# Moving query tiles into the kv stage and output weights to another queue in a fused gated-mix kernel

## The chip, the cores and the metric

The kernel runs on one core of one Trainium2 chip. The metric is the device time of one execution in microseconds (us); where several executions were measured, the median is given. A profiled execution records every instruction of every engine, with the clock that was granted to TensorE; positions in it are given in us from the start of its span.

## The reference, cut to what matters

The input is one sequence of S = 2048 tokens with D = 512 features in bf16. Two branches are computed from it and mixed by a gate:

```python
g = sigmoid((x * gate_w).sum(-1, keepdims=True))
# A: linear attention, 32 heads of width 16
q, k, v = split(x @ wqkv)
pq, pk = q @ w_phi, k @ w_phi                        # per head
phi_q = concat(softmax(pq), softmax(-pq))            # 32 features
phi_k = concat(softmax(pk), softmax(-pk))
kv, z = phi_k^T v, sum_s phi_k                       # over all tokens
a = ((phi_q kv) / (phi_q z + 1e-6)) @ wo
# B: gated MLP that mixes tokens
zz = gelu(x @ w_in); z1, z2 = zz[:, :688], layernorm(zz[:, 688:])
b = (z1 * (w_sp @ z2 + b_sp)) @ w_out
out = g * a + (1 - g) * b
```

## The kernel before, in words

The tokens are cut into 16 tiles of 128 rows. The kernel has three stages.

**The z stage** (to about 49 us) computes both gelu halves of branch B (`z_mm`, line 184) and the layer norm of the second, and folds `w_phi` into the query and key weights.

**The kv stage** (lines 495 to 513, from about 49 to 120 us) loops over the 16 tiles. An iteration computes the key features of the next tile (`k_tile`: four matmuls on line 318, two exps on ScalarE on line 322, the softmax sums on VectorE on line 326, reciprocals and a ratio, and a rescaling of the negative half on GpSimd on line 335), the values of this tile (`v_tile`, lines 358 to 363), adds the kv product of the tile two iterations back into one accumulator (`kv_acc`, line 374), and computes one "spatial half" of branch B (`gg_next`: 16 matmuls on line 410 for one half of the columns of one tile of `w_sp @ z2`, then the gating by z1 on VectorE on line 415). After both halves of a tile the product is transposed by a DMA transpose (`u_T`, line 441). Iterations 13 and 15 also compute a query tile (`q_tile`): the same steps as a key tile and then a DMA transpose into `eqT` (line 352). After the loop, the last kv products are added and the accumulator is masked into `kvz` (lines 380 and 385).

**The output stage** (lines 516 to 527) first loads the output weights (`load_out_weights`: a memset on GpSimd and five DMA loads into one tile, `slabs`, which takes the space of the key and value weights). Then 16 slots follow. Slot i computes query tile i+2, one spatial half, attention tile i (`attn_tile`: eight matmuls on line 423, the division on VectorE on lines 426 and 428, a DMA transpose of the result on line 436), and in odd slots from 3 on the output of a pair of tiles (`ba_pair`: for each tile four matmuls on line 447 with `wo`, five on line 449 and a last one on line 452 with `w_out`, a scaling on ScalarE, and the store). The last two output tiles stand alone, the last one in two halves of the columns.

What sets the order: TensorE and ScalarE run in the order of the code (`manual_schedule`). On VectorE, GpSimd and SP a scheduler fixes the order when the kernel is built; each engine then runs its own list strictly in order, the DMA issues on SP's and ScalarE's lists among the rest. All DMA transposes are on SP. Buffers are rings: six PSUM banks for `mm`, one accumulator shared by `kvacc` and `at`, two buffers for `eq`, four for `eqT`, ten for `uT`, four for `oT`, four for the gate products `ucat`. A writer waits until its buffer's last reader is done.

Of the kernel before, what the change touches and what calls it, by code (L numbers as in the profile page):

```python
# [11 lines left out]
BF16 = mybir.dt.bfloat16  # L12
I32 = mybir.dt.int32

P = 128
# [5 lines left out]
FH = 688  # L21
HF = FH // 2
NT = S // P
# [3 lines left out]
NFT = (FH + P - 1) // P  # L27
# [3 lines left out]
REM = FH - 5 * P  # L31
# [4 lines left out]
def kernel(  # L36
# [14 lines left out]
    nc = tc.nc  # L51
# [15 lines left out]
    wq_p = pers.tile([P, NDT, D], BF16, name="wq_p")  # L67
# [39 lines left out]
        out=ramp[:, 0, :], data0=ones32[:, :], data1=zeros[:, :], initial=0.0,  # L107
# [4 lines left out]
    for q in range(4):  # L112
        qs = slice(32 * q, 32 * q + 32)
        nc.vector.tensor_tensor(
            out=ident[qs, qs], in0=ramp[qs, 0, :], in1=ramp[qs, 1, :], op=ALU.is_equal)
    nc.gpsimd.dma_start(out=gaterow[:, :], in_=gate_w.rearrange("(dt p) -> dt p", p=P))
    nc.gpsimd.dma_start(out=brow[:, :], in_=B_b_sp.rearrange("(t p) -> t p", p=P))
    def load_z2w(eng, dt):
# [9 lines left out]
        out=xs[:, 2:4, :], in_=x2[2 * P:4 * P, :].rearrange("(i p) d -> p i d", p=P))  # L128
    for h in range(2):
        nc.sync.dma_start(  # L130
            out=w_z1[:, 2 * h:2 * h + 2, :], in_=w_in_v[:, 2 * h:2 * h + 2, 0:FH])
    for i in range(4, 8):
        nc.sync.dma_start_transpose(out=xT[:, :, i * P:(i + 1) * P], in_=x2[i * P:(i + 1) * P, :])
    for q in range(2, NCH):
        nc.sync.dma_start_transpose(
            out=xT[:, :, q * CH:(q + 1) * CH], in_=x2[q * CH:(q + 1) * CH, :]
# [4 lines left out]
        out=wv_sb[:, :, :],  # L141
        in_=A_wqkv[:, 2 * D:3 * D].rearrange("(dt p) n -> p dt n", p=P),
    )
    for q in range(NCH):
        nc.sync.dma_start_transpose(
            out=wspT[:, :, q * CH:(q + 1) * CH], in_=B_w_sp[q * CH:(q + 1) * CH, :]
# [4 lines left out]
        out=eexp[:, :], in_=eexp[:, :], pattern=[[0, 8], [-1, 16]],  # L151
# [4 lines left out]
        out=mask_bd[:], in_=mask_bd[:], pattern=[[-16, 8], [0, 16]],  # L156
# [3 lines left out]
        out=mask_bd[:], in_=mask_bd[:], pattern=[[16, 8], [0, 16]],  # L160
# [4 lines left out]
        out=mask4[:], in_=mask4[:], pattern=[[-32, NG]],  # L165
# [3 lines left out]
        out=mask4[:], in_=mask4[:], pattern=[[32, NG]],  # L169
# [3 lines left out]
        out=mask64[:, :, :], in_=mask4[:, :, None].to_broadcast([P, NG, DH]))  # L173
# [134 lines left out]
    work = ctx.enter_context(tc.tile_pool(name="work", bufs=2, reuse_waits="tile"))  # L308
# [3 lines left out]
    def mm_tile():  # L312
        return psM.tile([P, CH], FP32, name="mm", tag="mm", bufs=6)

    def expo(pool, name, bufs, tt, w):
        ps = mm_tile()
        for dt in range(NDT):
            nc.tensor.matmul(ps[:, :], lhsT=xT[:, dt, tt * P:(tt + 1) * P], rhs=w[:, dt, :],  # L318
                             start=(dt == 0), stop=(dt == NDT - 1))
        e = pool.tile([P, H, 2, DH], BF16, name=name, bufs=bufs)  # L320
        for a in range(2):
            nc.scalar.activation(  # L322
                out=e[:, :, a, :], in_=ps[:, :].rearrange("p (h f) -> p h f", f=DH),
                func=AF.Exp, scale=1.0 - 2.0 * a)
        z = work.tile([P, H, 2], FP32, name="zs")
        nc.vector.tensor_reduce(  # L326
            out=z[:].rearrange("p h a -> p (h a)"), in_=e[:].rearrange("p h a f -> p (h a) f"),
            axis=AX.X, op=ALU.add,
        )
        return e, z  # L330

    def even_out(e, z, rz):
        ratio = work.tile([P, H], FP32, name="ratio")
        nc.vector.tensor_tensor(out=ratio[:], in0=z[:, :, 0], in1=rz, op=ALU.mult)  # L334
        nc.gpsimd.tensor_tensor(  # L335
            out=e[:, :, 1, :], in0=e[:, :, 1, :],
            in1=ratio[:, :, None].to_broadcast([P, H, DH]), op=ALU.mult)

    def k_tile(tt):
        ek, z = expo(kvp, "ek", 5, tt, wk_p)  # L340
        rk = kvp.tile([P, H, 2], FP32, name="rk", bufs=3)
        nc.vector.reciprocal(out=rk[:], in_=z[:])
        even_out(ek, z, rk[:, :, 1])
        return ek, rk

    def q_tile(tt):
        eq, z = expo(work, "eq", 2, tt, wq_p)
        rq = work.tile([P, H], FP32, name="rq")
        nc.vector.reciprocal(out=rq[:], in_=z[:, :, 1])
        even_out(eq, z, rq[:])  # L350
        eqT = work.tile([P, 8, P], BF16, name="eqT", bufs=4)
        nc.sync.dma_start_transpose(out=eqT[:, :, :], in_=eq[:].rearrange("p h a f -> p (h a f)"))
        eqTs[tt] = eqT

# [36 lines left out]
    def load_out_weights():  # L391
        slabs = outw.tile([P, 11 + NDT, D], BF16, name="slabs")
        w_main = [slabs[:, 0:5, :], slabs[:, 5:10, :]]
        w_rem, wo_t = slabs[:, 10, :], slabs[:, 11:11 + NDT, :]
        nc.gpsimd.memset(w_rem, 0.0)
        nc.sync.dma_start(out=wo_t, in_=A_wo.rearrange("(g p) n -> p g n", p=P))
        for i in range(2):
            nc.sync.dma_start(
                out=w_main[i],
                in_=B_w_out[i * REM:i * REM + 5 * P, :].rearrange("(ft p) n -> p ft n", p=P),  # L400
            )
        nc.sync.dma_start(out=w_rem[0:REM, :], in_=B_w_out[5 * P:FH, :])
        nc.sync.dma_start(out=w_rem[P - REM:P, :], in_=B_w_out[0:REM, :])
        return w_main, w_rem, wo_t

    def gg_half(tt, j):
# [30 lines left out]
        oTs[tt] = oT  # L437

    def u_T(tt):
        uT = work.tile([P, NFT, P], BF16, name="uT", bufs=10)  # L440
        nc.sync.dma_start_transpose(out=uT[:, :, :], in_=ucat[tt % NU][:, :])
        return uT

    def ba_main(acc, tt, c0=0, c1=D):
        oT, uT, i = oTs[tt], uTs[tt], tt % 2
        for g in range(NG):
            nc.tensor.matmul(acc, lhsT=oT[:, g, :], rhs=wo_t[:, g, c0:c1], start=(g == 0), stop=False)  # L447
        for ft in range(5):
            nc.tensor.matmul(acc, lhsT=uT[:, i + ft, :], rhs=w_main[i][:, ft, c0:c1], start=False, stop=False)  # L449

    def ba_rem(acc, tt, rows, c0=0, c1=D):
        nc.tensor.matmul(  # L452
            acc, lhsT=uTs[tt][rows, 5 * (1 - tt % 2), :], rhs=w_rem[rows, c0:c1], start=False, stop=True)

    def ba_store(acc, tt, c0, c1, on_dve):
        ob = work.tile([P, c1 - c0], BF16, name=f"ob{c1 - c0}")
        dst = out2[tt * P:(tt + 1) * P, c0:c1]
        if on_dve:
            nc.vector.tensor_scalar(  # L459
                out=ob[:, :], in0=acc, scalar1=g_inv[:, tt:tt + 1], scalar2=None, op0=ALU.mult)  # L460
            nc.sync.dma_start(out=dst, in_=ob[:, :])
        else:
            nc.scalar.activation(out=ob[:, :], in_=acc, func=AF.Copy, scale=g_inv[:, tt:tt + 1])  # L463
            nc.scalar.dma_start(out=dst, in_=ob[:, :])
# [9 lines left out]
    def ba_pair(p):  # L474
        accs = [mm_tile() for _ in range(2)]
        for s_ in range(2):
            ba_main(accs[s_][:, :], 2 * p + s_)
        for s_ in range(2):
            ba_rem(accs[s_][:, :], 2 * p + s_, halves[s_])
        for s_ in range(2):  # L480
            ba_store(accs[s_][:, :], 2 * p + s_, 0, D, False)

    oTs = {}
    uTs = {}
    eqTs = {}
    ggs = [(tt, j) for tt in range(NT) for j in range(2)]

    def gg_next():
        tt, j = ggs.pop(0)
        gg_half(tt, j)  # L490
        if j == 1:
            uTs[tt] = u_T(tt)

    with tc.manual_schedule(engines={mybir.EngineType.PE, mybir.EngineType.Activation}):
        ks = {0: k_tile(0)}
        kvacc = psM.tile([P, 8, P], FP32, name="kvacc", tag="kvat", bufs=1)
        pend = []
        for tt in range(NT):
            if tt + 1 < NT:
                ks[tt + 1] = k_tile(tt + 1)  # L500
            ek, rk = ks.pop(tt)
            pend.append((tt, ek, v_tile(tt, rk)))
            if len(pend) == 3:
                kv_acc(*pend.pop(0))
            gg_next()
            if tt in (13, 15):
                q_tile((tt - 13) // 2)
        nc.scalar.activation(out=g_el[:, :], in_=glog[:, :], func=AF.Exp)
        nc.vector.tensor_scalar(out=g_1p[:, :], in0=g_el[:, :], scalar1=1.0, scalar2=None, op0=ALU.add)
        nc.vector.reciprocal(out=g_inv[:, :], in_=g_1p[:, :])  # L510
        for p_ in pend:
            kv_acc(*p_)
        kvz_evac()
        kvp_cm.__exit__(None, None, None)
        kvw_cm.__exit__(None, None, None)
        outw = ctx.enter_context(
            tc.tile_pool(name="outw", bufs=1, side="right", reuse_waits="tile"))
        w_main, w_rem, wo_t = load_out_weights()
        for i in range(NT):
            if i + 2 < NT:  # L520
                q_tile(i + 2)
            gg_next()
            attn_tile(i)
            if i >= 3 and i % 2 == 1:
                ba_pair((i - 3) // 2)
        ba_tile(14)
        ba_tile(15, nsplit=2)

# [29 lines left out]
```

## Time and profile before

| | before |
|---|---|
| median of 13 executions | 214.07 us (213.41 to 216.9) |
| the profiled execution's own time | 216.9 us |
| its span, first to last instruction | 215.2 us |
| mean granted TensorE clock | 0.992 |
| busy TensorE, VectorE, ScalarE, GpSimd | 207.3, 128.4, 73.7, 46.6 us |
| one spatial half: 16 matmuls (line 410), start to start | 2.33 us |
| query or key tile: 4 matmuls (line 318), start to start | 0.86 us |
| softmax sum (line 326) | 1.21 us |
| exp (line 322), one of two | 0.59 us |
| rescaling on GpSimd (line 335) | 1.06 us |
| DMA transposes eqT, oT, uT, issue to landing, median | 3.4, 2.9, 2.8 us |
| output weights, issue to landing | 3.9 us (wo), 6.4 us (the two large parts) |

How to read the lines: a row of the timeline has the start, the duration, the engine, the line of the kernel, the operation, output and inputs, and in brackets how long the engine was idle before it and what released it. "PE" is TensorE's matmuls, "PEld" its weight loads, "SPq" and "ACTq" are DMA issues by SP and ScalarE. Matmuls are pipelined: the distance from start to start is what a series costs, and a single one's duration is longer. A row of the windows by one engine has the stretch, its length, the busy time, the granted clock, the busy share of the DMA engines and GB/s. The page's row of 40 slices has one digit for each 5.38 us, in tenths.

### The profile page before, as it was taken

Reading aid. Unit: us, or ns where it says so; the run is one execution under the profiler, and the core shown is the slowest. Engines: PE = TensorE matmul, PEld = TensorE weight load, DVE = VectorE, ACT = ScalarE, POOL = GpSimd, SP = SyncE. Lnnn points to the kernel's source line nnn. Section 1 sums busy time; section 2 is a strip of 40 time slices with the busy share of each in tenths; the row PEclk is TensorE's granted clock in tenths of the full one; section 3 lists DMA queues with packets and bytes.
Section 4 is the critical chain, followed back from the end, with each engine's and each line's share of the span. In section 5 each row is a group of like instructions: output and inputs, shape, how many; then the busy total and the mean of one; then the engine's idle time right before and its main releaser. Section 6 shows DMA issues by size and latency. Waiting matters only on the chain.

```text
span 215.2 us, 3745 instructions
## 1 busy us (share of the span) xinstructions
PE 207.3 (96%) x1437; PEld 123.0 (57%) x1456; DVE 128.4 (60%) x284; ACT 73.7 (34%) x119; POOL 46.6 (22%) x77
## 2 busy tenths in 40 slices
PE   8999999999999999999999959999999999999993
PEld 3566666665566656665656635555554646464642
DVE  3194686764977766776678835819091647364500
ACT  2156656668232223222330403242322324141122
POOL 7002202020442233224224211112111111111000
PEclk9999999999999999999999996999999999999999
DMA  6999999999922010110211699591827673749732
GB/s 196 258 205 171 210 269 186 269 277 200 271 43 40 2 37 12 29 37 0 41 37 36 145 249 201 98 173 38 170 45 103 124 149 86 133 100 96 163 85 75
DMA packets 88994, 27.20 MB, mean 126 GB/s; under 512 B 82864, under 2 KB 88976, under 8 KB 88976
## 3 DMA queue, kind: packets, MB, share of 16 engines
q1 hardware_dynamic: 85648, 24.38, 60.4%
q10 hardware_dynamic: 3264, 2.58, 4.2%
q8 instruction: 11, 0.18, 0.4%
q14 instruction: 7, 0.06, 0.1%
q0 software_dynamic: 64, 0.01, 0.0%
HBM read 4.41 MB, written 2.10 MB: 30 GB/s over the span
## 4 chain that ended last, share of the span: by engine, by line
PE 91%; DMA 5%; DVE 2%; issue 1%; SPq 0%
PE mm L410 34%; PE zp L184 18%; PE mm L318 12%; PE mm L449 8%; PE mm L358 6%; PE mm L447 6%; DMA xs<-in_A_x_dram 2%; DMA eqT<-eq 2%; PE kvacc L374 2%; PE at L423 2%; PE mm L452 1%; DVE zs L326 1%; PE fps L265 1%; PE tp L233 0%; DVE ob L459 0%
## 5 line engine op out<-in xcount | busy, mean ns | idle before, releaser
L410 PE MATMUL mm<-z2all,wspT 128*128 128x344 bf16 x512 | 81.5, 313 | 0.3
L410 PEld LDWEIGHTS <-wspT 128*128 128x128 bf16 x512 | 49.6, 99 | 26.6 <-issue 0.4
L184 PE MATMUL zp<-w_z,xT 128*128 128x344 bf16 (+1 forms) x256 | 41.6, 318 | 0.0
L326 DVE TENSOR_REDUCE zs<-eq 128x64 f32<-128x1024 bf16 x16 | 19.5, 1216 | 31.2 <-ACT eq L322 31.2
L184 PEld LDWEIGHTS <-xT 128*128 128x128 bf16 x256 | 24.8, 100 | 11.8 <-DVE xT L235 0.2
L322 ACT ACTIVATE ek<-mm 128x512 bf16<-128x512 f32 x32 | 17.3, 596 | 40.4 <-PE mm L318 40.4
L335 POOL TENSOR_TENSOR eq<-eq,ratio 128x512 bf16<-128x512 bf16 x16 | 16.9, 1058 | 60.2 <-DVE ratio L334 49.8
L322 ACT ACTIVATE eq<-mm 128x512 bf16<-128x512 f32 x32 | 17.4, 594 | 31.9 <-DMA eqT<-eq 15.3
L463 ACT ACTIVATE ob<-mm,g_inv 128x512 bf16<-128x512 f32 (+1 forms) x16 | 10.8, 674 | 42.9 <-PE mm L452 39.9
L415 DVE SCALAR_TENSOR_TENSOR ucat<-mm,bT,z1all 128x344 bf16<-128x344 f32 x32 | 18.1, 566 | 9.8 <-PE mm L410 9.5
L326 DVE TENSOR_REDUCE zs<-ek 128x64 f32<-128x1024 bf16 x16 | 19.2, 1208 | 2.8 <-ACT ek L322 2.8
L449 PE MATMUL mm<-slabs,uT 128*128 128x512 bf16 (+1 forms) x85 | 20.1, 367 | 0.0
L363 DVE TENSOR_TENSOR vr<-mm,rk 128x512 bf16<-128x512 f32 x16 | 11.0, 686 | 11.9 <-PE mm L358 11.9
L318 PEld LDWEIGHTS <-xT 128*128 128x128 bf16 x128 | 11.5, 97 | 10.9 <-issue 1.3
L335 POOL TENSOR_TENSOR ek<-ek,ratio 128x512 bf16<-128x512 bf16 x16 | 16.9, 1059 | 2.1 <-DVE ratio L334 0.6
L447 PE MATMUL mm<-slabs,oT 128*128 128x512 bf16 (+1 forms) x65 | 16.4, 366 | 0.2
L358 PE MATMUL mm<-wv_sb,xT 128*128 128x512 bf16 x64 | 16.4, 379 | 0.0
L196 ACT ACTIVATE z2all<-zp 128x688 bf16<-128x688 f32 x16 | 11.9, 744 | 13.1 <-PE zp L184 13.1
L318 PE MATMUL mm<-wk_p,xT 128*128 128x512 bf16 x57 | 15.9, 379 | 0.4
L318 PE MATMUL mm<-wq_p,xT 128*128 128x512 bf16 x55 | 15.3, 381 | 0.2
L199 DVE BATCH_NORM_STATS2 bn<-z2all 128x6 f32<-128x344 bf16 x32 | 14.9, 502 | 0.0
L204 ACT ACTIVATE z1all<-zp 128x688 bf16<-128x688 f32 x16 | 11.9, 744 | 6.9 <-PE zp L184 6.9
(73 smaller groups left out, 143.8 us busy)
## 6 DMA issues: line engine op xcount, KB each, us to landing
out_dram<-ob ACTq DMA_DIRECT2D x15, 128.0 KB, 2.6
slabs<-in_B_w_out_dram SPq DMA_DIRECT2D x2, 640.0 KB, 6.4
w_z<-in_B_w_in_dram SPq DMA_DIRECT2D x2, 344.0 KB, 4.9
w_z<-in_B_w_in_dram ACTq DMA_DIRECT2D x3, 172.0 KB, 3.4
wv_sb<-in_A_wqkv_dram SPq DMA_DIRECT2D x1, 512.0 KB, 4.8
slabs<-in_A_wo_dram SPq DMA_DIRECT2D x1, 512.0 KB, 3.9
xs<-in_A_x_dram SPq DMA_DIRECT2D x2, 128.0 KB, 4.1
xs<-in_A_x_dram SPq DMA_DIRECT2D x1, 256.0 KB, 5.4
```

What stands on the lines that cost most here:

```text
L184: nc.tensor.matmul(zp[:, j, 0:n], lhsT=xT[:, dt, tt * P:(tt + 1) * P], rhs=wt[:, dt, j * HF:j * HF + n], start=(dt == 0), stop=(dt == NDT ...
L196: nc.scalar.activation(out=z2v, in_=zp[:, :, 0:HF], func=AF.Gelu_apprx_tanh)
L199: nc.vector.bn_stats(out=bn6[:, tt, j, :], in_=z2v[:, j, :])
L318: nc.tensor.matmul(ps[:, :], lhsT=xT[:, dt, tt * P:(tt + 1) * P], rhs=w[:, dt, :], start=(dt == 0), stop=(dt == NDT - 1))
L322: nc.scalar.activation(out=e[:, :, a, :], in_=ps[:, :].rearrange("p (h f) -> p h f", f=DH), func=AF.Exp, scale=1.0 - 2.0 * a)
L326: nc.vector.tensor_reduce(out=z[:].rearrange("p h a -> p (h a)"), in_=e[:].rearrange("p h a f -> p (h a) f"), axis=AX.X, op=ALU.add,)
L335: nc.gpsimd.tensor_tensor(out=e[:, :, 1, :], in0=e[:, :, 1, :], in1=ratio[:, :, None].to_broadcast([P, H, DH]), op=ALU.mult)
L358: nc.tensor.matmul(v_ps[:, :], lhsT=xT[:, dt, tt * P:(tt + 1) * P], rhs=wv_sb[:, dt, :], start=(dt == 0), stop=(dt == NDT - 1))
L410: nc.tensor.matmul(gp[:, 0:HF], lhsT=wspT[:, st, tt * P:(tt + 1) * P], rhs=z2all[:, st, j * HF:(j + 1) * HF], start=(st == 0), stop=(st == ...
L415: nc.vector.scalar_tensor_tensor(out=ucat[tt % NU][:, c0 + j * HF:c0 + (j + 1) * HF], in0=gp[:, 0:HF], scalar=bT[:, tt:tt + 1], in1=z1all[ ...
L447: nc.tensor.matmul(acc, lhsT=oT[:, g, :], rhs=wo_t[:, g, c0:c1], start=(g == 0), stop=False)
L449: nc.tensor.matmul(acc, lhsT=uT[:, i + ft, :], rhs=w_main[i][:, ft, c0:c1], start=False, stop=False)
```

## The change

It moves and re-buffers work; no computation is added or removed.

- Six query tiles (0 to 5) are computed in the kv stage, after iterations 5, 7, 9, 11, 13 and 15, where before there were two (after 13 and 15). In the output stage, slot i then computes query tile i+6 instead of i+2.
- `eq` has three buffers instead of two, `eqT` eight instead of four, `uT` nine instead of ten.
- Iteration 0 of the kv stage computes no spatial half; it is computed after the kv stage, ahead of the output weights and slot 0.
- The five loads of the output weights are issued by ScalarE instead of SP.
- A slot starts with its attention tile; the query tile and the spatial half follow.
- Output pairs stand in slots 2, 4, ... 14 instead of 3, 5, ... 15.

```diff
     def q_tile(tt):
-        eq, z = expo(work, "eq", 2, tt, wq_p)
+        eq, z = expo(work, "eq", 3, tt, wq_p)
...
-        eqT = work.tile([P, 8, P], BF16, name="eqT", bufs=4)
+        eqT = work.tile([P, 8, P], BF16, name="eqT", bufs=8)
...
-        nc.sync.dma_start(out=wo_t, in_=A_wo.rearrange("(g p) n -> p g n", p=P))
+        nc.scalar.dma_start(out=wo_t, in_=A_wo.rearrange("(g p) n -> p g n", p=P))
         for i in range(2):
-            nc.sync.dma_start(
+            nc.scalar.dma_start(
...
-        nc.sync.dma_start(out=w_rem[0:REM, :], in_=B_w_out[5 * P:FH, :])
-        nc.sync.dma_start(out=w_rem[P - REM:P, :], in_=B_w_out[0:REM, :])
+        nc.scalar.dma_start(out=w_rem[0:REM, :], in_=B_w_out[5 * P:FH, :])
+        nc.scalar.dma_start(out=w_rem[P - REM:P, :], in_=B_w_out[0:REM, :])
...
-        uT = work.tile([P, NFT, P], BF16, name="uT", bufs=10)
+        uT = work.tile([P, NFT, P], BF16, name="uT", bufs=9)
...
+    Q_AT = (5, 7, 9, 11, 13, 15)
...
-            gg_next()
-            if tt in (13, 15):
-                q_tile((tt - 13) // 2)
+            if tt > 0:
+                gg_next()
+            if tt in Q_AT:
+                q_tile(Q_AT.index(tt))
...
+        gg_next()
         w_main, w_rem, wo_t = load_out_weights()
+        nq = len(Q_AT)
         for i in range(NT):
-            if i + 2 < NT:
-                q_tile(i + 2)
-            gg_next()
             attn_tile(i)
-            if i >= 3 and i % 2 == 1:
-                ba_pair((i - 3) // 2)
+            if i + nq < NT:
+                q_tile(i + nq)
+            if ggs:
+                gg_next()
+            if i >= 2 and i % 2 == 0:
+                ba_pair((i - 2) // 2)
         ba_tile(14)
         ba_tile(15, nsplit=2)
```

## The prediction

> **What bounds the kernel now.** I read the page first: engine totals and the row of 40 slices, then the waits of TensorE, then the timeline and half-microsecond windows around the one wait that mattered.
>
> The engine totals and the granted clock (each digit is a slice of 5.38 us):
>
> ```profile
> PE 207.3 (96%) x1437; PEld 123.0 (57%) x1456; DVE 128.4 (60%) x284; ACT 73.7 (34%) x119; POOL 46.6 (22%) x77
> PEclk9999999999999999999999996999999999999999
> ```
>
> TensorE is busy for 207.3 of 215.2 us, so only idle TensorE time or a slow clock can be won. One digit, the 25th (129.1 to 134.5 us), is 6. All that TensorE waited for, in total, times, longest:
>
> ```profile
> PE at L423 <- DMA eqT<-eq: 2.2, 1, 2.2
> PE zp L226 <- PEq L542: 0.8, 1, 0.8
> PE tp L233 <- DMA xs<-in_A_x_dram: 0.4, 1, 0.4
> ```
>
> One wait, 2.2 us, is inside the work: an attention tile waits for the transposed query features. The rest is the start; the end (last matmul at 211.85, span 215.2) is the last store. The timeline shows how the wait arises:
>
> ```profile
> 119.09 0.67 PE L374 MATMUL kvacc<-vr,ek 128*128 128x68 bf16 x16
> 119.80 0.69 DVE L380 TENSOR_TENSOR kvz<-kvacc,mask 128x512 bf16<-128x512 f32 x1 [0.80 <-PE kvacc L374]
> ...
> 120.42 0.46 SPq L396 DMA_DIRECT2D slabs<-in_A_wo_dram  x1
> 120.92 0.50 SPq L398 DMA_DIRECT2D slabs<-in_B_w_out_dram  x1
> ...
> 121.62 0.18 DVE L385 SCALAR_TENSOR_TENSOR kvz<-kvacc,mask 128x32 bf16<-128x32 f32 x1
> ...
> 123.59 1.23 SPq L352 DMA_TRANSPOSE eqT<-eq  x1
> ...
> 128.58 0.43 PE L423 MATMUL at<-kvz,eqT 128*128 128x68 bf16 x8 [2.17 <-DMA eqT<-eq]
> ...
> 129.77 4.12 PE L410 MATMUL mm<-z2all,wspT 128*128 128x344 bf16 x16
> ```
>
> The kv sum ends at T = 119.76. Query tile 1, computed just before T, is transposed only at 123.59, behind 1152 KB of output weights on the same queue; it lands at 128.54 (4.95 us; median of the 16 is 3.4) and attention tile 1 starts at 128.58 after 2.17 us of nothing. The next spatial half (L410) takes 4.12 instead of 2.50 us. The windows say why:
>
> ```profile
> 129.00:129.50 0.50, 0.50 (x5) 1.00 1.10 354
> 130.00:130.50 0.50, 0.50 (x3) 0.50 1.22 256
> 132.50:133.00 0.50, 0.50 (x4) 0.50 0.34 69
> 133.50:134.00 0.50, 0.50 (x12) 1.00 0.88 170
> ```
>
> The third number is the clock: half from 129.67 to 133.07 (finer windows place the edges), 3.40 us. The wait costs 2.17 itself and 4.12 - 2.50 = 1.62 after it: 3.79 us.
>
> **The change, part by part.**
>
> *Six query tiles in the kv stage.* No instruction is added: four more query tiles (2 to 5) move ahead of T. On TensorE each is 4 matmuls of 0.86 us together (start to start), 3.44 us moved, sum 0. What the wait needs is gone: tiles 0 to 5 are transposed long before attention, and tile 6, computed in slot 0, is used in slot 6. Gain 2.17, and the half clock with it.
>
> What each moved tile brings into the kv stage: ScalarE two exps of 0.594; VectorE 1.216 + 0.336 + 0.168 = 1.72; GpSimd 1.06; SP one transpose issue of 1.25. Without a query tile, an iteration of kv takes TensorE 4.31 and VectorE 1.21 + 0.54 + 0.27 + 0.69 + 0.57 = 3.28 us. Two iterations with one query tile: TensorE 8.62 + 0.86 = 9.48, VectorE 6.56 + 1.72 = 8.28. That is 87%, so TensorE still bounds. In the built order VectorE takes both sums (query, key) before the v scaling; in the trace that pattern exists once, at tile 0 (108 to 117 us): v scaling starts 114.76, 2.4 us after its matmuls end, and TensorE shows no gap. The consumers, kv products, come two iterations (about 9 us) later, and the six accumulator banks come round after 6 us or more. Cost 0; bounds 0 and, should VectorE sums run 15% longer (9.5 us), a stall of the excess per pair of iterations. GpSimd (1.27 x 2 + 1.06 of 9.48) and SP (two issues, 2.5 of 9.48) are far from full.
>
> *One spatial half moved from kv iteration 0 to just after T.* Sum 0 on TensorE. At the start, key product 0 comes 2.33 us earlier, at about 57.2; its last input, GpSimd's rescaled tile (end 56.68), precedes it by 0.5. At T, before, a query tile and a spatial half (0.86 + 2.33 us) covered the evacuation of the kv sum, which ended at 121.80 = T + 2.04. Now only the spatial half does; VectorE's order there is as before. Margin 0.3; cost 0, at worst 0.3.
>
> *Weights from ScalarE's queue.* The five issues took 0.46 + 0.50 + 0.58 + 0.56 + 0.93 = 3.03 us on SP. On ScalarE they start at the same point (T + 0.66, after the memset) and end at T + 3.7. Queued behind them are the exps of query tile 6, whose matmuls end at T + 2.33 + 0.25 + 0.86 = T + 3.4: delayed by 0.3, and nobody needs them before slot 6. SP gains 3.03 us for transposes. What covers the transfer: output pair 0 now starts after the half and three slots of 0.25 + 0.86 + 2.33, at T + 12.65 (before, 137.43 = T + 17.7). The last issue starts at T + 2.76; the slowest landing of the five was 6.8, so T + 9.6. Cover 3 us.
> Here a rule of the Trainium skill speaks against the move ("DMA: Bandwidth & Descriptors", "Issuing engines are not separate DMA queues"): transfers from any engine share the same DMA engines, so only issue time is saved. By it the weights would still crowd the transposes and, had the query tiles not moved, most of the 4.95 us would stay; by the row, the gain comes from tile 1 being early. I book nothing for the queue.
>
> *Pairs at even slots, and the end.* Seven pairs as before. A pair now needs the attention output of the slot before: 0.86 + 2.33 + 0.25 + 0.86 + 2.33 + 1.94 = 8.57 us between attention tile i-1 and its use; the way there is about 1.4 on VectorE and 2.9 for issue and landing: 4.5. In the slots without query tiles it is 6.85 against 4.5. No cost.
> But the order at the end changes. Before, pair 6 (4.3 us) and tile 14 stood between the last spatial half and tile 15. Now pair 6 is in slot 14, and only tile 14 remains. From the start of the last half: half 2.33, tile 14 2.17 (207.34 to 209.51), the attention part of tile 15 0.44: tile 15 wants its transposed gate product at 4.94. That one comes, by the last half of before, at: first matmul 200.45, VectorE done 203.57, issue 203.59, landing 2.8: 206.39, or 5.94. Stall 1.00. Bounds: 0.9 (landing 2.7) and 2.7 (landing 4.5, slowest seen). Value 1.0: nothing large is on the queues there.
>
> *Half clock.* Its worth in other executions is the open term. The skill ("TensorE: Matmul & The Clock Gate", Part 1) has the clock halved after an idle window of some 3.4 us, the window running free of the program. By the rule taken at its word, 2.17 us of idling cost no clock and the removal is worth 2.17. By the row, 2.17 idle out of the 3.40 us before the dip (64%, the whole wait inside one window) sufficed: 3.79. If half a window idle is enough, a window of 3.40 at random phase has at least 1.70 of a wait of 2.17 in (3.40 - 2.17 + 2 x 0.47) / 3.40 = 64% of executions; I book 0.64 x 1.62 = 1.04 as an estimate, bounds 0 and 1.62. The stall at the end, 1.0 in 3.4, is well under that share: no dip.
>
> *Larger buffers* (eq 3, eqT 8, uT 9): tiles 0 to 8 of uT are the nine live ones when pair 0 frees two. 0.
>
> **Sum.** Against the profiled execution: 216.9 (span 215.2, 1.7 around it) - 2.17 - 1.62 + 1.00 = 214.1. The profile is 2.8 us over the median of 214.07, so it is not the median's execution, and the dip may be part of that. Against the median: 214.07 - 2.17 - 1.04 + 1.00 = 211.9.
>
> **Rivals.**
> A. The gap closes but the median never had the dip: 214.07 - 2.17 + 1.0 = 212.9. For it: the excess of 2.8 needs a cause. Against: the mechanism is a row of the trace. Full dip: 211.3.
> B. The end takes it all: landing 4.5 (stall 2.7) and no dip: 214.6; with dip, 213.0. For: tile 14's stores and the last transposes fall together. Against: 2.8 for the same transfer before, amid the same stores.
> C. Slower: pair 0 waits for the weights, now due 5 us earlier. It decides from a landing of T + 14.8: a stall of 2.2 would, by the row above, halve the clock too, 3.8 together, more than the 2.2 gained: 215.7. If they come when pair 0 used to start (T + 17.7): 211.9 + 5.0 + 1.6 = 218.5. Against: 3 us of cover, transposes of tiles 0 and 1 gone from that stretch.
> D. VectorE bounds the kv stage (over 9.48 per two iterations): five to six pairs, 0.5 each beyond that, 2.5 to 3: 214.6.
>
> **Chances.** Forecast with its dip between half and full 0.50; A 0.22; B 0.12; C 0.08; D 0.08. Faster by over 0.3% (below 213.4, about what a measurement of this kernel can tell): the forecast, A and a part of B, 0.75. Within: B and a mild D, 0.13. Slower: 0.12. The range goes from 210.7 (full dip, stall at the end half hidden) to 213.6.
>
> **What would show it.** In the profile after: no wait at L423, no 6 in the clock row; a wait at L449 of about 1 us at the last tile, for DMA uT; first pair without a wait on slabs; VectorE at about 87% from kv iteration 5 on, with TensorE still full. A wait at L447 or L449 near T + 12.65, or TensorE gaps before T, would prove me wrong.

## The result, and the profile after

The changed kernel takes 211.63 us (median of 11 executions, 211.24 to 212.22) against 214.34 us before (now over 48 executions). The ratio is 0.9876, 95% interval 0.9855 to 0.9896: 2.7 us less, with 211.9 forecast. Executions more than 1.5% above the fastest of their kernel count as slow and are left out of the ratios, and the one profiled before, at 216.9 us, is such a one. The profiled execution of the changed kernel has a span of 209.7 us.

From the page of the changed kernel, engine totals and granted clock:

```profile
PE 203.1 (97%) x1437; PEld 121.3 (58%) x1456; DVE 131.6 (63%) x284; ACT 73.2 (35%) x119; POOL 46.4 (22%) x77
PEclk9999999999999999999999999999999999999999
```

The 6 in the clock row is gone. What TensorE waits for now:

```profile
PE zp L226 <- PEq L547: 0.8, 1, 0.8
PE mm L449 <- DMA uT<-ucat: 0.8, 1, 0.8
PE tp L233 <- DMA xs<-in_A_x_dram: 0.5, 1, 0.5
```

No attention tile waits. The new wait is at the place that was forecast: the last output tile, for its transposed gate product. The timeline of the changed kernel, at the change of stages and at the end:

```profile
117.74 0.67 PE L374 MATMUL kvacc<-vr,ek 128*128 128x68 bf16 x16
120.65 0.42 PE L423 MATMUL at<-kvz,eqT 128*128 128x68 bf16 x8
124.10 0.42 PE L423 MATMUL at<-kvz,eqT 128*128 128x68 bf16 x8
127.55 0.42 PE L423 MATMUL at<-kvz,eqT 128*128 128x68 bf16 x8
131.00 1.03 PE L447 MATMUL mm<-slabs,oT 128*128 128x512 bf16 x4
...
201.68 1.21 SPq L441 DMA_TRANSPOSE uT<-ucat  x1
203.12 0.61 PE L447 MATMUL mm<-slabs,oT 128*128 128x256 bf16 x4
204.50 0.72 PE L449 MATMUL mm<-slabs,uT 128*128 128x256 bf16 x5 [0.77 <-DMA uT<-ucat]
```

Attention tiles 0 to 2 (L423) stand 3.45 us apart, which is the sum of the matmuls of a slot (0.25 + 0.86 + 2.33). Pair 0 starts 12.6 us after the end of the kv sum (T, here 118.41) and waits for nothing.

**The two first profiles must not simply be subtracted.** Their spans differ by 5.5 us, but the same code at the start accounts for 2.47 of it: the same series of 18 matmuls on line 184 begins at 10.93 before and at 8.46 after, because the first matmuls ran at half the pace for longer (six matmuls shortly ahead of that series took 1.88 us before and 1.04 after). The first line is from the trace before, the second from the trace after:

```profile
10.93 2.80 PE L184 MATMUL zp<-w_z,xT 128*128 128x344 bf16 x18
```
```profile
8.46 2.80 PE L184 MATMUL zp<-w_z,xT 128*128 128x344 bf16 x18
```

The granted clock reads 1.00 there in both, so the row does not show it. This start is chance: in the traces below the kv stage begins anywhere from 45.97 to 46.94, once at 47.53 and once at 50.71 us (these two also wait 1.1 and 1.4 us for the load of x). I therefore compare traces from T on.

### The profile page after: what moved, and what is told of

It reads as the page before. It is cut to its first block, busy times and chain, and to the rows that moved or that the text cites. A ratio compares the mean times of both kernels' runs of the same rounds, so it can differ in the third digit from the quotient of the medians.

```text
span 209.7 us, 3753 instructions
## 1 busy us (share of the span) xinstructions
PE 203.1 (97%) x1437; PEld 121.3 (58%) x1456; DVE 131.6 (63%) x284; ACT 73.2 (35%) x119; POOL 46.4 (22%) x77
## 4 chain that ended last, share of the span: by engine, by line
PE 94%; DMA 3%; issue 1%; DVE 1%; SPq 0%
PE mm L410 36%; PE zp L184 18%; PE mm L318 13%; PE mm L449 8%; PE mm L358 7%; PE mm L447 6%; PE at L423 2%; DMA xs<-in_A_x_dram 2%; PE kvacc L374 2%; DMA uT<-ucat 1%; PE mm L452 1%; PE fps L265 1%; PE tp L233 0%; DVE ucat L415 0%; DVE ob L459 0%
## 5 line engine op out<-in xcount | busy, mean ns | idle before, releaser
L410 PE MATMUL mm<-z2all,wspT 128*128 128x344 bf16 x512 | 79.8, 309 | 0.1
L410 PEld LDWEIGHTS <-wspT 128*128 128x128 bf16 x512 | 48.7, 98 | 24.1
L184 PE MATMUL zp<-w_z,xT 128*128 128x344 bf16 (+1 forms) x256 | 39.9, 309 | 0.2 <-DVE xT L235 0.2
L426 DVE RECIPROCAL rden<-at 128x32 f32<-128x32 f32 x16 | 5.4, 339 | 23.4 <-PE at L423 23.4
```

Of the source, the lines that this page charges most:

```text
L184: nc.tensor.matmul(zp[:, j, 0:n], lhsT=xT[:, dt, tt * P:(tt + 1) * P], rhs=wt[:, dt, j * HF:j * HF + n], start=(dt == 0), stop=(dt == NDT ...
L410: nc.tensor.matmul(gp[:, 0:HF], lhsT=wspT[:, st, tt * P:(tt + 1) * P], rhs=z2all[:, st, j * HF:(j + 1) * HF], start=(st == 0), stop=(st == ...
```

## The experiments

The theory at the outset: the wait at tile 1 (2.2 us) and the half clock behind it are what was won, and the end gives 1 us back. Rivals: it was the weights in SP's queue; the half clock belonged to one profile only; VectorE binds the kv stage. Times are medians; "before" is measured on the same chip in each comparison.

**1. Query tiles alone** (`q6_alone`, repeated as `q6_again`): the kernel before with

```diff
-            if tt in (13, 15):
-                q_tile((tt - 13) // 2)
+            if tt in Q_AT:                       # (5, 7, 9, 11, 13, 15); eq 3, eqT 8 buffers
+                q_tile(Q_AT.index(tt))
...
-            if i + 2 < NT:
-                q_tile(i + 2)
+            if i + len(Q_AT) < NT:
+                q_tile(i + len(Q_AT))
```

> The kernel before with one part of the change alone: six query tiles in the kv stage (eq 3, eqT 8 buffers), slots, pairs and weight queue as before. My theory: the wait at attention tile 1 (2.17 us) and the half clock after it (1.62) go, and nothing is given back at the end, since the last pair still stands there: 214.3 - 3.8 = 210.5 us, 1.1 below the changed kernel. Rival (the half clock was only in that one profile): 212.2. Rival (VectorE binds the kv stage): above 213, with TensorE gaps before the end of kv.

> The kernel before with six query tiles in the kv stage alone, again, since the first measurement spread over 2 us: 211.7 to 212.3, that is 2.0 to 2.6 below before: the waits at the attention tiles (2.8 us) gone, 0.8 back at the output of tile 1, whose transpose stands behind SP's weight issues.

Measured 212.26 us, ratio 0.9913 (0.9882 to 0.9945), and 211.83, ratio 0.991 (0.9877 to 0.9942). Not the 210.5 of my theory; near the rival without a half clock. The attention tiles no longer wait for query features, but a new wait comes in its place (0.8 us in the first trace), here from the trace of the repeat:

```profile
PE mm L447 <- DMA oT<-o: 1.2, 1, 1.2
PE at L423 <- DVE o L428: 0.3, 1, 0.3
```

The attention output of tile 0 is transposed late, behind SP's last weight issues, and that of tile 1 waits for its buffer. So one part of the change gets about 1.9 of the 2.7 us, and the queue matters after all. The edit also gives `eq` its third buffer; what that alone would do was not tried.

**2. Weights on ScalarE's queue alone** (`act_weights_alone`): the kernel before with the five `nc.sync.dma_start` of `load_out_weights` as `nc.scalar.dma_start`.

> The kernel before with the five weight loads on ScalarE's queue alone. My theory: the DMA engines are shared, so tile 1's transpose still meets the weights and attention tile 1 still waits, perhaps 1 to 2 us; also the exps of query tile 2, queued behind 3 us of issues, come 2.8 us later, and attention tile 2 may wait about 1 us: 213 to 215 us. Rival (the weights ahead on the same queue were the cause): no wait at tile 1, 210.5 to 212.

Measured 219.76 us, ratio 1.0261 (1.0226 to 1.0295): about 5.6 us slower, and worse than I expected. From its timeline:

```profile
121.33 1.24 SPq L352 DMA_TRANSPOSE eqT<-eq  x1
128.02 0.43 PE L423 MATMUL at<-kvz,eqT 128*128 128x68 bf16 x8 [3.87 <-DMA eqT<-eq]
128.76 2.28 DVE L326 TENSOR_REDUCE zs<-eq 128x64 f32<-128x1024 bf16 x2
129.15 4.17 PE L410 MATMUL mm<-z2all,wspT 128*128 128x344 bf16 x16
132.82 2.63 SPq L352 DMA_TRANSPOSE eqT<-eq  x2
136.07 0.64 PE L423 MATMUL at<-kvz,eqT 128*128 128x68 bf16 x8 [2.75 <-DMA eqT<-eq]
```

Tile 1's transpose, issued at 121.33, now lands after 6.6 us instead of 4.95. All five weight loads are issued ahead of it, where before three of them came only behind it; that it meets more of them is the likely reason, not a measured one. That the weights still hold it up from another queue is what the Trainium skill says ("DMA: Bandwidth & Descriptors", "Issuing engines are not separate DMA queues": the engines are shared whoever issues), and the rival that the queue caused the wait at tile 1 falls. The second wait is an order effect: the exps of tile 2 stand behind the issues on ScalarE, and on VectorE's list its softmax sum now stands behind the reciprocal of attention tile 1; the sum at 128.76 had to wait for that late tile. After each wait the clock halves (the spatial half at 129.15 takes 4.17 us), and all six executions have a mean clock of 0.982 to 0.992. In this kernel, then, moving the weights can help only where no query tile is due in those microseconds.

**3. The half clock by itself** (`filler`): the kernel before with about 2.2 us of TensorE work in the wait; it adds matmuls whose result nobody reads.

```diff
             gg_next()
+            if i == 1:
+                fl = mm_tile()
+                for _ in range(10):
+                    nc.tensor.matmul(fl[:, :], lhsT=xT[:, 0, 0:P], rhs=wq_p[:, 0, :], start=True, stop=True)
             attn_tile(i)
```

> The kernel before with ten matmuls of 512 columns, whose result nobody reads, put ahead of attention tile 1: 2.16 us of TensorE work inside the wait of 2.17. It measures the half clock by itself. If the dip belongs to the median execution: the wait is filled, no half clock, 214.3 - 1.6 = 212.7 us. If it was only in the profile: 214.3. If the estimate of 64 per cent holds: about 213.3. If the wait is shorter in executions without a profile: above 214.3.

Measured 214.47 us against 214.09, ratio 1.0021 (1.0002 to 1.0041): nothing won. A mean clock of 0.992 or less shows in 1 of its 22 executions, in 7 of the 27 beside it of the kernel before. So the filler seems to have kept the clock up (the counts are small), and the median execution had nothing to gain from that. Its trace held a surprise, in slot 2:

```profile
130.39 0.41 PE L423 MATMUL at<-kvz,eqT 128*128 128x68 bf16 x8 [0.66 <-DVE o L428]
```

This led to a new theory: without the half clock the kernel before waits twice, and the half clock, where it falls, hides the second wait.

**4. A second trace of the kernel before** (`before_again`), unchanged.

> The kernel before once more, for a second trace. In the filler run no execution lost clock to the wait, and yet nothing was won; its trace has a wait of 0.7 us at attention tile 2. New theory: without the half clock, the kernel before waits at tile 1 and again at tile 2 (together about 2.9 us), and the half clock, where it falls, hides the second wait. Expected: a start of the kv stage near 46.4 us instead of 48.8, a wait of 2.2 at tile 1, no half clock, a wait of 0.5 to 0.8 at tile 2. Rival: the half clock is there again with 1.6 us, and the start alone made the first profile long.

This execution took 214.20 us (span 212.5), so it is like the median. Its timeline:

```profile
117.24 0.67 PE L374 MATMUL kvacc<-vr,ek 128*128 128x68 bf16 x16
120.95 0.42 PE L423 MATMUL at<-kvz,eqT 128*128 128x68 bf16 x8
126.55 0.43 PE L423 MATMUL at<-kvz,eqT 128*128 128x68 bf16 x8 [1.99 <-DMA eqT<-eq]
127.68 2.50 PE L410 MATMUL mm<-z2all,wspT 128*128 128x344 bf16 x16
129.94 1.09 ACT L322 ACTIVATE eq<-mm 128x512 bf16<-128x512 f32 x2 [2.25 <-DMA eqT<-eq]
130.15 0.41 PE L423 MATMUL at<-kvz,eqT 128*128 128x68 bf16 x8
134.45 0.43 PE L423 MATMUL at<-kvz,eqT 128*128 128x68 bf16 x8 [0.69 <-DMA eqT<-eq]
```

The spatial half behind the wait takes its normal 2.50 us: no half clock. And there is a second wait, in slot 3 rather than slot 2: the exps of the following query tiles wait for `eq` buffers held by delayed transposes (2.25 us at 129.94), so the delay travels on. Attention tiles are 5.60, 3.60 and 4.30 us apart where 3.44 is the work: 3.18 us lost in this one trace, 0.5 more than the bracketed idle times. The difference is in how a series is drawn: a spatial half lasts 2.50 us, but the matmul behind it normally starts 2.33 us after its start. That overlap of 0.17 is lost at each of the three late tiles, and the brackets do not count it.

Over the 57 executions of the kernel before in the comparisons of these experiments, 16 have a mean clock of 0.992 or less; their median is 214.82 (214.72 without the four above 216), that of the other 41 is 213.87. The two traces of the kernel before say the same: from T on, the one with the half clock takes 95.4 us, the one without 94.6. The half clock costs about 0.9 net, in a quarter of the executions. None of the 18 executions of the changed kernel, `after_again` with it, has a mean clock below 0.997.

**5. The end** (`after_odd_pairs`, `after_late_pair6`; `after_again` is the changed kernel beside the latter):

```diff
-            if i >= 2 and i % 2 == 0:
-                ba_pair((i - 2) // 2)
+            if i >= 3 and i % 2 == 1:                  # after_odd_pairs
+                ba_pair((i - 3) // 2)
```
```diff
-            if i >= 2 and i % 2 == 0:
+            if i >= 2 and i % 2 == 0 and i < 14:       # after_late_pair6
                 ba_pair((i - 2) // 2)
+        ba_pair(6)
         ba_tile(14)
```

> The changed kernel with the output pairs back at odd slots. My theory: the last pair stands again between the last spatial half and tile 15, so the wait for uT at the end (0.77 us by the profile of the changed kernel, and 0.2 for oT just ahead) goes: 211.6 - 0.9 = 210.7 us. Rival (the wait at the end is hidden by the stores that follow anyway): 211.6.

> The changed kernel once more, to stand beside the two variants of it on one chip: 211.6 us.

> The changed kernel with its last output pair (tiles 12 and 13) moved behind the last spatial half; all other pairs stay at even slots. My theory: 4.3 us of work cover the last transpose, the wait of 0.77 (and the 0.2 ahead of it) goes: 0.9 below the changed kernel, 210.7 us. Rival: the end is set by something else (the stores), no change.

Odd pairs gave 210.96 us, ratio 0.987 (0.9834 to 0.9905), with executions from 210.27 to 212.26: its interval does not separate it from the changed kernel. Its trace has no wait at the end, but one of 0.3 us for VectorE at an attention tile. The cleaner edit did better: 210.33 us, ratio 0.9819 (0.9782 to 0.9855), beside 211.64 and 0.9876 (0.9837 to 0.9915) for the changed kernel again. All that TensorE waits for in it is the start:

```profile
PE zp L226 <- PEq L548: 0.8, 1, 0.8
PE tp L233 <- DMA xs<-in_A_x_dram: 0.3, 1, 0.3
PE zp L184 <- DVE xT L235: 0.2, 1, 0.2
```

From T to the end of the span it takes 90.2 us, the changed kernel in that comparison 91.2. So the reordered end costs the change 1.0 us by the traces and 1.3 by the medians. The intervals of the two ratios meet, but each of the six executions is shorter than each of the six beside it. This version is the best measured here, below the kernel before and the changed one.

**6. The queue, inside the changed kernel** (`after_sp_weights`): the changed kernel with the five loads back on `nc.sync`.

> The changed kernel with the five weight loads back on SP. By my prediction the queue is worth nothing here: 211.6 us. By the trace of the run with six query tiles alone, where the output of tile 1 waited 0.8 us for its transpose behind SP's five issues: a wait of 0.5 to 3 us at the first pair, which now starts 5 us earlier: 212.2 to 214.6.

Measured 212.43 us, ratio 0.9917 (0.9892 to 0.9943), against 0.9876 for the changed kernel: about 0.8 us worse, though the two intervals touch. The trace has the reason, a wait for a transposed attention output, once 0.37 us at pair 0 and once 0.56 at the end:

```profile
PE mm L447 <- DMA oT<-o: 0.9, 2, 0.6
```
```profile
126.09 0.57 SPq L398 DMA_DIRECT2D slabs<-in_B_w_out_dram  x1
127.79 1.19 SPq L436 DMA_TRANSPOSE oT<-o  x1
131.97 1.04 PE L447 MATMUL mm<-slabs,oT 128*128 128x512 bf16 x4 [0.37 <-DMA oT<-o]
```

From T on it takes 91.9 us instead of 91.2 to 91.3. Only the wait at pair 0 counts in that: pair 0 starts at T + 13.1 instead of T + 12.6. The wait at the end stands in place of the one for the gate product; from the last spatial half to the last matmul it is 7.6 us in both kernels. My prediction had booked nothing for the queue.

**7. How many query tiles, and how dense** (`late6_q3`, `late6_dense`): the kernel of `after_late_pair6` with

```diff
-    Q_AT = (5, 7, 9, 11, 13, 15)
+    Q_AT = (11, 13, 15)                        # late6_q3
+    Q_AT = (10, 11, 12, 13, 14, 15)            # late6_dense
```

> The changed kernel with its last pair behind the last half, and three query tiles (after iterations 11, 13 and 15) in the kv stage instead of six. My theory: what counts is that tile 1 is not computed just before the weights; with three tiles of lead, tile 3 (computed in slot 0) has 17 us until slot 3, and its way took about 12 in the changed kernel: no wait, 210.3 us as with six. Rival (depth is needed, because ScalarE's weight issues and VectorE's fixed order delay the first query tiles of the output stage): a wait of 1 to 3 us at attention tile 3, 211.3 to 213.3.

> The changed kernel with its last pair behind the last half, and its six query tiles after six iterations in a row (10 to 15) instead of every second one: VectorE then has 5.0 us of work in each iteration of 5.18 on TensorE. It tests the rival that VectorE binds the kv stage. If only VectorE's sum matters: 97 per cent, no loss, 210.3 us. If its fixed order with two softmax sums ahead of the v scaling leaves it idle while it waits for exps: 0.3 to 1 us lost per iteration, 212 to 216, with TensorE gaps at L374 or L318 before the end of the kv stage.

Three tiles gave 212.12 us, ratio 0.9907 (0.9877 to 0.9937), above the six tiles of either other version (210.33, and 210.73 on the same chip); my theory was wrong. The wait is not at tile 3 but at tile 2:

```profile
120.86 1.24 SPq L352 DMA_TRANSPOSE eqT<-eq  x1
127.60 0.43 PE L423 MATMUL at<-kvz,eqT 128*128 128x68 bf16 x8 [1.31 <-DMA eqT<-eq]
```

Whatever their number, the last query tile of the kv stage is computed just before T and transposed while the weights come in. Issued at about T + 3.8 in every trace, it took 6.5 to 7.7 us in the seven with the weights on ScalarE's queue, and 3.6 to 4.9 in the six with them on SP's. With two tiles it is wanted in slot 1, with three in slot 2 (still 1.3 too early), with six in slot 5. That trace also starts its kv stage later (47.53 against 46.29), so its whole time misleads. From T on, less the three query tiles that did not move ahead of it, it takes 91.7 us against the 90.2 of `after_late_pair6`: 1.5 us, the wait of 1.31 and its lost overlap.

Six tiles in a row gave 210.73 us, ratio 0.985 (0.9822 to 0.9879); the interval overlaps that of the 210.33 with every second iteration, and from its first key matmul to the last kv products the kv stage takes 71.42 us in both traces. A window of its late kv stage, and one of the changed kernel over two iterations (stretch, length, then busy time and count of TensorE, weight loads, VectorE, ScalarE, GpSimd):

```profile
110.00:116.00 6.00, 5.95 (x51) 3.81 (x51) 6.00 (x10) 1.62 (x4) 2.28 (x4) 1.00 0.38 71
```
```profile
79.94:89.43 9.49, 9.44 (x68) 5.59 (x68) 7.97 (x14) 3.15 (x6) 3.56 (x5) 1.00 0.30 57
```

VectorE is busy for all of 6.00 us and TensorE still does not wait: the buffers between them hold. In the changed kernel VectorE is at 84% of two iterations. The rival that VectorE binds the kv stage falls.

## Why the prediction was right

The time was right to 0.3 us, and the mechanism was right: the gap closes and the end gives 1 us back. But two of the terms were mis-sized in opposite directions and a third was missing, so that the sum came out so close is luck.

- **The wait at tile 1: right, but only one part of what was lost.** Booked 2.17. The median-like execution loses 3.18 in the first slots: the wait at tile 1, one at tile 3, and the lost overlap. I had read a trace in which the second wait was hidden by the half clock, and took the trace's single wait for all there is.
- **Half clock: mis-sized.** Booked 0.64 x 1.62 = 1.04. It falls in 16 of 57 executions (28%) and costs 0.9 net, for the reason just given; the median hardly holds it. The step that failed is the assumption that half an idle window is enough. Waits of about 2 us, 60% of the 3.40 us of the dip, set it off in a quarter of the executions. So few executions leave room for 17 to 41%: not for the 64% booked, but for the 36% in which, by the prediction's own arithmetic, such a wait would lie wholly inside one window. The rule of the Trainium skill ("TensorE: Matmul & The Clock Gate", Part 1) has the clock halve after at least one idle window of some 3.4 us. For the median execution that came nearer than my estimate. As a threshold it does not hold here, since the clock did fall after 2.17 us of idling in the first trace, and after 2.75 at the second wait of experiment 2.
- Together: booked 2.17 + 1.04 = 3.21, measured 3.18 and, over many executions, 0.28 x 0.9 = 0.25 of the half clock. The errors cancelled. Rival A, that the median never had the dip, was near the truth in that; its 212.9 was too high because it too lacked the second wait.
- **The end: right.** Booked -1.00. The trace has 0.94 at the gate product (203.12 to 204.50 for matmuls of 0.44) and 0.08 just ahead; undoing it gave 1.0 by the traces.
- **Weights on ScalarE's queue: wrong.** Booked 0. In the changed kernel it is worth about 0.6 by the traces and 0.8 by the medians; left alone it costs 5.6. What I missed is SP's own time: with three issues of weights left between the transposes, the attention outputs are issued later, and pair 0 now asks for them one slot earlier. Without this part the change came out at 212.43. (The way of the attention output, put at 4.5, adds up to 4.3; nothing hangs on it.)
- **The kv stage: right.** From its first key matmul to the last kv products it takes 70.30 us before and 71.42 after; the difference of 1.12 is what moved, 4 x 0.86 - 2.33. Rival D, VectorE as the bound, falls with it.
- **Covers: right, thinner than booked.** Pair 0 at T + 12.6 (12.65 booked). The slowest weight load took 8.1 us, not 6.8, so about 2 us of cover were left of the 3. The evacuation of the kv sum ended at 120.50, and attention tile 0 started at 120.65, 0.06 us later than the matmuls ahead of it would have had it: just in time.

From T on the changed kernel takes 91.3 us and the median-like execution before 94.6, of which 1.1 only moved ahead of T: 2.2 won (3.18 - 1.02). The medians say 2.7, interval 2.2 to 3.1. Whether the rest is the half clock in a quarter of the executions or the start of the kernel, whose chance differences are as large, is not settled. Rival C did not come about, since pair 0 waited for nothing; what late weights would cost was not tried. Nor were the larger buffers, the spatial half moved out of iteration 0 and the new order within a slot tried by themselves.

## What to carry to other kernels

A producer-consumer chain that ends in a DMA transpose should not be computed last before a bulk load: what helped here is that the consumer comes several slots later. Another queue alone made it worse, and one tile more of lead left a wait of 1.3 us. When work is moved to close a gap in the middle, look at what it leaves uncovered at the end: two lines that put the last pair back behind the last spatial half gave another 1.0 us. And a single profile can hide a second wait behind the consequence of the first; a second trace of the same kernel, before any arithmetic, would probably have shown both that and the chance at the start.

## What the runs showed of the hardware that was not expected

- The clock is halved in some executions and not in others after a wait of 2 us: in 16 of 57 executions, for 3.40 us where it was traced, at a net cost of 0.9 us.
- A transpose of 256 KB within SBUF lands in about 3 us at its fastest. With weights ahead on its own queue it took 3.6 to 4.9 us in six traces, and with all the weights coming on the other queue 6.5 to 7.7 us in seven: a second queue made it slower.
- A wait of TensorE costs about 0.17 us more than the idle time in the trace, for the overlap of two series (2.50 us long, 2.33 us apart) that it loses.
- The first matmuls of an execution run at half pace for a time that varies between executions of the same code, by 2.47 us of delay between the two first traces, while the granted clock reads 1.00.
